# Last group of layer 1: activation left in PSUM, gh by ScalarE, weight patterns one step sooner and their low parts on two engines

## The chip, the cores and the metric

The kernel runs on one core of one Trainium2 chip. The metric is the device time of one execution in microseconds. The engines are named as in the profile: PE is TensorE (matmuls), DVE is VectorE, ACT is ScalarE, POOL is GpSimd, and SP is SyncE, which only issues transfers here.

## The reference

Three stages follow one another. The first is a linear attention with a decaying state over 768 positions, for 4 sequences and 8 heads of 48 channels:

```python
cur = np.einsum('bhd,bhe->bhde', u[None] * kt, vt)
y[:, :, t] = np.einsum('bhd,bhde->bhe', rt, state + cur)
state = w[None, :, :, None] * state + np.einsum('bhd,bhe->bhde', kt, vt)
```

Its result, 3072 tokens by 384 channels, goes through two layers of the same shape (384 to 2048 to 384) with two activations:

```python
h = x @ w_in;  g = h * (1.0 / (1.0 + np.exp(-1.702 * h)));  x = g @ w_out        # layer 1
h = x @ w_in;  sp = np.log1p(np.exp(np.minimum(h, 20.0)));  out = (h * np.tanh(sp)) @ w_out   # layer 2
```

The weights come as 64-bit floats, all the rest as 32-bit floats.

## The kernel before

**Precision.** A 32-bit operand is split in two: a high part, which is a copy rounded to the format of PE's faster 32-bit matmul, and a low part, which is the operand minus the high part. A product is then three matmuls: high by high, low by high, high by low (`PASSES`).

**Weights.** The two matrices of a layer are cut into 16 tiles of 128 partitions by 768 columns. `Layer` brings one tile in five steps. `fetch` loads the raw 64-bit words (SP issues it). `bits` puts together the 32-bit pattern from the two halves of each word, in three DVE instructions: part 0 (L110), part 1 (L116), part 2 (L119). `high` (L142, ACT) copies the pattern into the high part, `low` (L149, POOL) subtracts. A loaded raw tile lies in one of three buffers (two of the tag `raw`, one of `x2_5`), a pattern in one of two of the tag `wv`, and the parts in one of 16 buffers, which the 16 tiles of layer 1 fill: tile m of layer 2 gets its place when tile m of layer 1 was used for the last time.

**Order.** The schedule is manual: each engine runs its instructions in the order of the program, and a wait stands where an instruction needs a result or a buffer of another engine. The tokens are worked through in 6 groups of 512. For a group and a tile m, `product_in` (L544, 9 matmuls) makes h(m) in one of two PSUM buffers, the activation gives g(m), it is split into gh and gl, and `product_out` (L657, 9 matmuls) adds it to three accumulators in PSUM. In groups 0 to 4 of layer 1 the loop also carries the attention of later tokens (units A, kv, y, the masks L385 and the diagonals L358), and in groups 1 to 4 the range check of the weights: each tile of both layers is loaded a second time and read by two ACT instructions, L133 and L135, one in each step, 64 in all.

**The last group of layer 1** (the loop at L751 and after, g = 5) has no attention. In its step m PE runs `product_in` of m and, from m = 1 to 13, `product_out` of m - 1 (`close_tile`); tiles 13 to 15 are closed behind the loop. ACT writes the activation to SBUF (gf, L767), DVE makes gh (a cast, L768) and gl (L769). In the same steps the weights of layer 2 are prepared: `bits` of m - 1, `high` and `low` of m - 2, `fetch` of m + 1. In steps 6, 8 and 10 one third of the first group's input of layer 2 is split (`split_x2`, L581 on DVE and L582 on POOL).

**Layer 2** (`Second`) goes by units u = 16 g + m, in pairs. `inp` makes k(u) into one of the same two PSUM buffers and reads it with ACT (s, L496) and DVE (y, L497); `act` does the rest of the activation for a pair (L506 and L507 on ACT with a change of tables before each, L508 on DVE); `split`, one pair later, gives bh (L520) and bl (L521); `out` (L534) is the second product, four units behind. The tags `s`, `y`, `gh` and `gl` have two buffers each of 128 by 1024. The order at the start is k(0), k(1), `product_out` of tiles 13 to 15, k(2), k(3), and then one k and one out in turn. `late_work` says what else is issued behind which unit: here `bits`, `high` and `low` of the tiles 13 to 15 that are left, and the split of the next group.

Of the kernel before, what the change touches and what calls it, by code (L numbers as in the profile page):

```python
# [17 lines left out]
P = 128  # L18
# [7 lines left out]
NF = 16  # L26
# [9 lines left out]
NB = 2  # L36
# [18 lines left out]
class Layer:  # L55
# [27 lines left out]
    def bits(self, m, part=None):  # L83

        if not 0 <= m < NF:
            return
        if part is None:
            for k in range(3):
                self.bits(m, k)
            return  # L90
        V = self.nc.vector
        raw = self.raw[m]
        if not self.wide:
            self.v[m] = raw
            return
        if part == 0:
            pool, tag, bufs = self.patslot(m)
            self.v[m] = pool.tile([P, 768], I32, tag=tag, name=f"wv{self.tag}_{m}", bufs=bufs)
        v = self.v[m]
        L, H = raw[:, :, 0], raw[:, :, 1]  # L100
        if part == 0:
            if self.general:
                V.tensor_scalar(out=v, in0=H, scalar1=0x7FFFFFFF, scalar2=None, op0=ALU.bitwise_and)
                V.tensor_scalar(out=v.bitcast(F32), in0=v.bitcast(F32), scalar1=F_MIN, scalar2=F_MAX,
                                op0=ALU.max, op1=ALU.min)
                V.tensor_scalar(out=v, in0=v, scalar1=4, scalar2=1, op0=ALU.logical_shift_left,
                                op1=ALU.logical_shift_right)
# [33 lines left out]
        w = self.t[m] = self.wpool.tile([P, 2, 768], F32R, tag="wt", name=f"w{self.tag}_{m}")  # L141
        self.nc.scalar.activation(out=w[:, 0, :], in_=self.v[m].bitcast(F32), func=AF.Copy)  # L142

    def low(self, m, half=None):
        if not 0 <= m < NF:
            return
        sl = slice(0, 768) if half is None else slice(384 * half, 384 * half + 384)
        w = self.t[m]
        self.nc.gpsimd.tensor_tensor(out=w[:, 1, sl], in0=self.v[m][:, sl].bitcast(F32), in1=w[:, 0, sl].bitcast(F32),  # L149
                                     op=ALU.subtract)  # L150

    def win(self, m, part, kt):
        return self.t[m][:, part, 128 * kt:128 * kt + 128]
# [395 lines left out]
def feed_forward(tc, ctx, ins, out, w_sb, chk, consts, general):  # L549
    nc = tc.nc  # L550
    chan, tok, wch, ub, w1, w2, cst = ins
    NG = len(GROUPS)
    starts = [sum(GROUPS[:g]) for g in range(NG)]
    V, A = nc.vector, nc.scalar

    wpool = ctx.enter_context(tc.tile_pool(name="wpool", bufs=NF))
    spool = ctx.enter_context(tc.tile_pool(name="spool", bufs=2))
    xpool = ctx.enter_context(tc.tile_pool(name="xpool", bufs=2))
    x2pool = ctx.enter_context(tc.tile_pool(name="x2pool", bufs=1))
    hpool = ctx.enter_context(tc.tile_pool(name="hpool", bufs=2, space=PSUM))  # L560

    late = {}

    l1 = Layer(nc, w1, wpool, lambda m: (x2pool, "x2_2", 1) if m % 3 == 2 else (spool, "raw", 2),
               lambda m: (x2pool, "x2_1" if m % 2 else "x2_3", 1), "a", chk, spool, general)
    l2 = Layer(nc, w2, wpool, lambda m: (late["x"], "x2_5", 1) if m % 3 == 1 else (spool, "raw", 2),
               lambda m: (late["x"], "wv", 2), "b", chk, spool, general)
    x2, xs, xs2 = {}, {}, {}

    def new_x(g, tag):  # L570
        n = GROUPS[g]
        return (xpool.tile([P, 3, n], F32R, tag="xh", name=f"xh{tag}{g}"),
                xpool.tile([P, 3, n], F32R, tag="xl", name=f"xl{tag}{g}"))

    def split_x2(g, z):
        if g >= NG:
            return
        if z == 0:
            xs2[g] = new_x(g, "b")
        xh, xl = xs2[g]  # L580
        V.tensor_copy(out=xh[:, z, :], in_=x2[g][:, z, :])  # L581
        nc.gpsimd.tensor_tensor(out=xl[:, z, :], in0=x2[g][:, z, :], in1=xh[:, z, :].bitcast(F32), op=ALU.subtract)  # L582


# [66 lines left out]
    def product_out(g, m, gt):  # L651
        n = GROUPS[g]
        if m == 0:
            acc[g] = [psum.tile([P, 512], F32, tag="acc", name=f"acc{g}_{z}", bufs=3) for z in range(3)]
        for ct in range(3):
            for k, (wz, gz) in enumerate(PASSES):
                nc.tensor.matmul(acc[g][ct][:, :n], lhsT=l1.wout(m, wz, ct), rhs=gt[gz],  # L657
                                 start=m == 0 and k == 0, stop=m == NF - 1 and k == 2,
                                 skip_group_check=True)

    def evacuate(g):
        n = GROUPS[g]
        x2[g] = (x2pool if g < NG - 2 else late["x"]).tile([P, 3, n], F32, tag=f"x2_{g}", name=f"x2_{g}")
        for ct in range(3):
            if ct == 0 or g == NG - 1:
                A.activation(out=x2[g][:, ct, :], in_=acc[g][ct][:, :n], func=AF.Copy)
            else:
                V.tensor_copy(out=x2[g][:, ct, :], in_=acc[g][ct][:, :n])

    def range_check(s):  # L670

        n = s // 2
        lay = lambda n: ((l1, l2)[n // NF], n % NF) if n < 2 * NF else (l2, NF)
        if s == 0:
            l1.check(0, 0)
            l1.check(1, 0)
        la, m = lay(n)
        la.check(m, 1 + s % 2)
        if s % 2 == 0 and n > 0:
            la, m = lay(n + 1)  # L680
            la.check(m, 0)

    pend = None
    d = BARE_TILES
    for g in range(NG - 1):
        n = GROUPS[g]
        for m in range(NF):
# [3 lines left out]
            h = product_in(nc, l1, m, xs[g], n, hpool, f"h{g}_{m}")  # L691
# [6 lines left out]
            gh = gpool.tile([P, n], F32R, tag="gh", name=f"gh{g}_{m}")  # L698
            gl = gpool.tile([P, n], F32R, tag="gl", name=f"gl{g}_{m}", bufs=1 if general else 2)
# [13 lines left out]
            if on and q == 2:  # L713
                unit_x(j)
                at.unit_t(j, 1, V)
                at.bonus(j + 1, 2, V)
            if g:
                range_check((g - 1) * NF + m)
            if g == 0:
                l1.bits(d, 2)  # L720
                d += 1
# [21 lines left out]
    g, n = NG - 1, GROUPS[-1]  # L743
# [4 lines left out]
    def close_tile(m):  # L748
        product_out(g, m, gts.pop(m))

    for m in range(NF):  # L751
        h = product_in(nc, l1, m, xs[g], n, hpool, f"h{g}_{m}")
        if m == 0:

            product_out(*pend)
            ax.close()
            late["x"] = ctx.enter_context(tc.tile_pool(name="x2late", bufs=1))
            bpool = ctx.enter_context(tc.tile_pool(name="bpool", bufs=2))
            evacuate(g - 1)
# [194 lines left out]
```

## Time and profile before

| | |
|---|---|
| median of 3 runs | 963.75 us (963.21 to 963.78) |
| the profiled execution | 960.98 us |
| its span | 959.1 us |
| PE busy | 912.9 us, 95% of the span |
| DVE busy | 501.6 us, 52% |
| ACT busy | 557.4 us, 58% |
| POOL busy | 232.8 us, 24% |
| data read, written | 74.37 MB, 4.72 MB |

The profiled execution is one of its own, and its time is larger than its span by what lies before the first and after the last instruction. Times inside the trace count from the start of the span. An engine's busy time is a mean over stages: attention with layer 1 to about 460 us, the last group of layer 1 to about 540, then layer 2.

### The profile page before, as it was taken

How to read it: one execution, taken by the hardware profiler on the slowest of the kernel's cores; microseconds unless marked ns; L12 is line 12 of the kernel's file. 1: busy time of each engine (PE TensorE's matmuls, PEld its weight loads, DVE VectorE, ACT ScalarE, POOL GpSimd, SP SyncE). 2: the span in 40 equal slices, each digit the busy share in tenths (PEclk: the TensorE clock that was granted, in tenths of full speed). 3: DMA queues.
4: the chain of work that ended last, by engine and by line, in shares of the span. 5: the costliest groups of instructions: out<-in, count | busy, mean ns of one | idle time of the engine just before them, and what ended most of it. 6: DMA issues, size and time to landing. Idle time of an engine off the chain costs nothing.

```text
span 959.1 us, 14032 instructions
## 1 busy us (share of the span) xinstructions
PE 912.9 (95%) x5702; PEld 768.1 (80%) x5702; DVE 501.6 (52%) x673; ACT 557.4 (58%) x869; POOL 232.8 (24%) x193
## 2 busy tenths in 40 slices
PE   4679999999999999999988999999999999999997
PEld 3557787887887877887866788999999999999986
DVE  6697842223322222322599867665555555555553
ACT  3445454556554555554322477777777777777773
POOL 5467743231223222221044202101001010010000
PEclk9799999999999999999999899999999999999999
DMA  8746434534334534322243200000000000000001
GB/s 224 220 144 205 141 108 135 140 122 136 112 107 131 153 114 132 115 92 89 109 162 134 98 1 1 1 33 1 1 33 1 33 1 1 33 1 1 33 1 38
DMA packets 30010, 80.09 MB, mean 84 GB/s; under 512 B 3056, under 2 KB 18672, under 8 KB 29936
## 3 DMA queue, kind: packets, MB, share of 16 engines
q1 hardware_dynamic: 29520, 78.66, 26.2%
q8 instruction: 47, 0.77, 0.3%
q10 hardware_dynamic: 416, 0.45, 0.2%
q14 instruction: 27, 0.22, 0.1%
HBM read 74.37 MB, written 4.72 MB: 82 GB/s over the span
## 4 chain that ended last, share of the span: by engine, by line
PE 80%; DVE 9%; issue 4%; POOL 3%; ACT 2%; DMA 2%; SPq 0%; POOLq 0%; DVEq 0%; ACTq 0%
PE bcc L534 20%; PE k L544 20%; PE acc L657 17%; PE h L544 16%; PE y L444 4%; DVE wvb L110 3%; PE A L381 2%; POOL wa L149 2%; DMA tkv<-in_tok_dram 2%; DVE wvb L116 1%; DVE wvb L119 1%; PE kv L418 1%; DVE bl L521 1%; POOL rkbuf L335 1%; DVE wva L119 0%
## 5 line engine op out<-in xcount | busy, mean ns | idle before, releaser
L534 PE MATMUL bcc<-wb,bh 128*128 128x384 f32 x768 | 211.5, 337 | 0.0
L657 PE MATMUL acc<-gh,wa 128*128 128x512 f32 x576 | 187.8, 407 | 3.7 <-DVE gh L768 3.7
L709 DVE TENSOR_TENSOR gl<-h,gh 128x512 fp32r<-128x512 f32 x80 | 55.3, 691 | 254.9 <-ACT gh L708 254.9
L544 PE MATMUL h<-xha,wa 128*128 128x512 f32 x576 | 180.4, 393 | 7.3 <-POOL wa L149 3.5
L544 PE MATMUL k<-xhb,wb 128*128 128x512 f32 x576 | 179.7, 393 | 2.2 <-ACT gf L767 2.2
L534 PEld LDWEIGHTS bcc<-wb,bh 128*128 128x128 f32 x768 | 140.3, 188 | 4.1
L707 ACT ACTIVATE h<-h 128x512 f32<-128x512 f32 x80 | 46.5, 581 | 163.0 <-PE h L544 163.0
L544 PEld LDWEIGHTS h<-xha,wa 128*128 128x128 f32 x576 | 108.5, 189 | 33.9 <-POOL wa L149 4.6
L657 PEld LDWEIGHTS acc<-gh,wa 128*128 128x128 f32 x576 | 106.1, 190 | 34.1 <-DVE gh L768 6.2
L534 PE MATMUL bcc<-wb,bl 128*128 128x384 f32 x384 | 129.2, 337 | 1.9 <-DVE bl L521 1.9
L544 PEld LDWEIGHTS k<-xhb,wb 128*128 128x128 f32 x576 | 106.8, 188 | 20.6 <-ACT gf L767 2.6
L657 PE MATMUL acc<-gl,wa 128*128 128x512 f32 x288 | 115.7, 402 | 4.3 <-DVE gl L769 2.9
L544 PE MATMUL k<-xlb,wb 128*128 128x512 f32 x288 | 114.1, 396 | 0.0
L544 PE MATMUL h<-xla,wa 128*128 128x512 f32 x288 | 112.9, 392 | 0.0
L497 DVE TENSOR_TENSOR y<-k,s 128x512 f32<-128x512 f32 x96 | 66.1, 691 | 86.3 <-ACT s L496 86.2
L508 DVE SCALAR_TENSOR_TENSOR y<-s,y 128x1024 f32<-128x1024 f32 x48 | 59.9, 1248 | 79.5 <-ACT s L507 79.5
L496 ACT ACTIVATE s<-k 128x512 f32<-128x512 f32 x96 | 57.3, 599 | 63.8 <-PE k L544 63.3
L582 POOL TENSOR_TENSOR xlb<-x,xhb 128x512 fp32r<-128x512 f32 x18 | 24.6, 1368 | 258.0 <-DVE xhb L581 258.0
L534 PEld LDWEIGHTS bcc<-wb,bl 128*128 128x128 f32 x384 | 72.1, 188 | 6.9 <-DVE bl L521 3.1
L506 ACT ACTIVATE s<-s,one 128x1024 f32<-128x1024 f32 x48 | 55.4, 1154 | 32.4 <-DVE y L497 32.3
L358 ACT ACTIVATE Am<-ident,a 128x128 f32<-128x128 f32 x192 | 58.5, 389 | 24.9 <-DVE a L348 24.9
L657 PEld LDWEIGHTS acc<-gl,wa 128*128 128x128 f32 x288 | 55.1, 191 | 20.3 <-DVE gl L769 5.6
(99 smaller groups left out, 1253.2 us busy)
## 6 DMA issues: line engine op xcount, KB each, us to landing
rawa<-in_w_dram SPq DMA_DIRECT2D x16, 768.0 KB, 4.5
chka<-in_w_dram SPq DMA_DIRECT2D x16, 768.0 KB, 4.4
chkb<-in_w_dram SPq DMA_DIRECT2D x16, 768.0 KB, 4.2
rawb<-in_w_dram SPq DMA_DIRECT2D x16, 768.0 KB, 4.1
rkbuf<-in_chan_dram SPq DMA_DIRECT2D x48, 192.0 KB, 5.5
tkv<-in_tok_dram SPq DMA_DIRECT2D x24, 384.0 KB, 6.1
tkr<-in_tok_dram SPq DMA_DIRECT2D x24, 192.0 KB, 5.7
out_dram<-o SPq DMA_DIRECT2D x10, 384.0 KB, 3.0
```

Of the source, the lines that this page charges most:

```text
L110: V.tensor_scalar(out=v, in0=H, scalar1=3, scalar2=0x3FFFFFF8, op0=ALU.logical_shift_left, op1=ALU.bitwise_and)
L358: self.nc.scalar.activation(out=am[:, z, p, :], in_=self.ident, func=AF.Copy, scale=self.a[j][:, 2 * p + z:2 * p + z + 1])
L444: self.nc.tensor.matmul(y[32 * s:32 * s + rows, C * x:C * x + C], lhsT=lhsT, rhs=rhs, start=n == 0, stop=n == len(jobs[s]) - 1, skip_group ...
L496: nc.scalar.activation(out=self.s[:, z, :n], in_=h[:, :n], func=AF.Sigmoid)
L497: nc.vector.tensor_tensor(out=self.y[:, z, :n], in0=h[:, :n], in1=self.s[:, z, :n], op=ALU.mult)
L506: nc.scalar.activation(out=s, in_=s, func=AF.Arctan, scale=-1.0, bias=self.one)
L508: nc.vector.scalar_tensor_tensor(out=y, in0=s, scalar=R2, in1=y, op0=ALU.add, op1=ALU.mult)
L534: self.nc.tensor.matmul(self.acc[g][t][:, :DM], lhsT=gt[gz][:, t * P:t * P + P], rhs=self.lay.wout(m, wz), start=m == 0 and k == 0, stop=m ...
L544: nc.tensor.matmul(h[:, :n], lhsT=lay.win(m, wz, kt), rhs=x[xz][:, kt, :], start=k == 0, stop=k == 8)
L657: nc.tensor.matmul(acc[g][ct][:, :n], lhsT=l1.wout(m, wz, ct), rhs=gt[gz], start=m == 0 and k == 0, stop=m == NF - 1 and k == 2, skip_grou ...
L707: A.activation(out=h[:, :n], in_=h[:, :n], func=AF.Gelu_apprx_sigmoid)
L709: V.tensor_tensor(out=gl, in0=h[:, :n], in1=gh.bitcast(F32), op=ALU.subtract)
```

## The change

- In the last group of layer 1 the activation is written back into h's PSUM buffer; ACT makes gh from it by a second instruction, and DVE makes gl from h (PSUM) and gh.
- `split_x2` in steps 6, 8 and 10 makes its high part on ACT.
- `bits` of tile m is done in step m, its parts 0 and 1 ahead of gl and part 2 behind it; all 16 patterns are made in the loop. `fetch` is issued for m + 3. `high` and `low` stay at m - 2 but are issued ahead of the activation; `low` is cut into two halves of 384 columns, the first on POOL, the second on DVE.
- The patterns of layer 2 lie in `wv` for m % 4 = 2, 3, and in the buffers of the tags `s` and `y` of layer 2 for m % 4 = 0, 1.
- In `late_work` the `bits` of tiles 14 and 15 are gone, and `high` and `low` of 14 and 15 come at units 7 and 9 instead of 9 and 11.
- The range checks of groups 1 to 4 go one in each step, but two in the steps 7 and 15 of a group, until the 64 are done.
- The second accumulator of group 4 is copied out by ACT instead of DVE.

```diff
-    def low(self, m, half=None):
+    def low(self, m, half=None, eng=None):
...
+        eng = eng or self.nc.gpsimd
         sl = slice(0, 768) if half is None else slice(384 * half, 384 * half + 384)
         w = self.t[m]
-        self.nc.gpsimd.tensor_tensor(out=w[:, 1, sl], in0=self.v[m][:, sl].bitcast(F32), in1=w[:, 0, sl].bitcast(F32),
-                                     op=ALU.subtract)
+        eng.tensor_tensor(out=w[:, 1, sl], in0=self.v[m][:, sl].bitcast(F32), in1=w[:, 0, sl].bitcast(F32),
+                          op=ALU.subtract)
...
     l2 = Layer(nc, w2, wpool, lambda m: (late["x"], "x2_5", 1) if m % 3 == 1 else (spool, "raw", 2),
-               lambda m: (late["x"], "wv", 2), "b", chk, spool, general)
+               lambda m: (late["x"], "wv", 2, 768) if m % 4 > 1 else (late["b"], "sy"[m % 4], 2, NB * 512), "b", chk, spool, general)
...
-        V.tensor_copy(out=xh[:, z, :], in_=x2[g][:, z, :])
+        if act:
+            A.activation(out=xh[:, z, :], in_=x2[g][:, z, :], func=AF.Copy)
+        else:
+            V.tensor_copy(out=xh[:, z, :], in_=x2[g][:, z, :])
...
-            if ct == 0 or g == NG - 1:
+            if ct == 0 or g == NG - 1 or (ct == 1 and g == NG - 2):
...
-            if g:
-                range_check((g - 1) * NF + m)
+
+            for _ in range(0 if g == 0 else 2 if m % 8 == 7 else 1):
+                range_check(checked)
+                checked += 1
...
         if m == 0:
 
+            A.activation(out=h[:, :n], in_=h[:, :n], func=AF.Gelu_apprx_sigmoid)
             product_out(*pend)
...
-            evacuate(g - 1)
...
-        gf = bpool.tile([P, NB, 512], F32, tag="s", name=f"gf{g}_{m}")[:, 0, :n]
+
+        if m < NF - 1:
+            l2.high(m - 2)
+            l2.low(m - 2, 0)
+            l2.low(m - 2, 1, V)
+        if m:
+            l2.bits(m, 0)
+            l2.bits(m, 1)
...
-        A.activation(out=gf, in_=h[:, :n], func=AF.Gelu_apprx_sigmoid)
-        V.tensor_copy(out=gh, in_=gf)
-        V.tensor_tensor(out=gl, in0=gf, in1=gh.bitcast(F32), op=ALU.subtract)
+        if m:
+            A.activation(out=h[:, :n], in_=h[:, :n], func=AF.Gelu_apprx_sigmoid)
+        A.activation(out=gh, in_=h[:, :n], func=AF.Copy)
+        if m == 0:
+            evacuate(g - 1)
+        V.tensor_tensor(out=gl, in0=h[:, :n], in1=gh.bitcast(F32), op=ALU.subtract)
         gts[m] = (gh, gl)
-        if m < NF - 1:
-            l2.bits(m - 1)
-            l2.high(m - 2)
-            l2.low(m - 2)
-            if m >= 2:
-                l2.fetch(m + 1)
+        if m == 0:
+            l2.bits(0)
+        else:
+            l2.bits(m, 2)
+        if m < NF - 3:
+            l2.fetch(m + 3)
         if 0 < m < NF - 2:
             close_tile(m - 1)
         if m in (6, 8, 10):
-            split_x2(0, m // 2 - 3)
+            split_x2(0, m // 2 - 3, True)
...
-    for u, f, *a in ((5, l2.high, 13), (5, l2.low, 13), (5, l2.bits, 14, 0), (5, l2.bits, 14, 1),
-                     (7, l2.bits, 14, 2), (7, l2.bits, 15, 0),
-                     (9, l2.high, 14), (9, l2.low, 14), (9, l2.bits, 15, 1), (9, l2.bits, 15, 2),
-                     (11, l2.high, 15), (11, l2.low, 15), (11, split_x2, 1, 0),
-                     (13, split_x2, 1, 1), (13, split_x2, 1, 2)):
+    for u, f, *a in ((5, l2.high, 13), (5, l2.low, 13), (7, l2.high, 14), (7, l2.low, 14), (9, l2.high, 15), (9, l2.low, 15),
+                     (11, split_x2, 1, 0), (13, split_x2, 1, 1), (13, split_x2, 1, 2)):
```

## Rows read from the trace of the kernel before

**Rows 1.** Windows: stretch, its length, busy time (count) by engine, PEclk, DMA, GB/s.

```profile
489.60:541.97 52.37, 43.55 (x164) 31.76 (x162) 51.05 (x52) 13.55 (x21) 22.49 (x13) 0.93 0.40 137
541.97:552.12 10.15, 10.12 (x37) 8.17 (x38) 6.36 (x8) 6.46 (x8) 1.44 (x1) 0.83 0.17 68
...
600.00:900.00 300.00, 300.00 (x1506) 271.71 (x1505) 170.07 (x214) 222.34 (x225) 18.15 (x14) 1.00 0.04 14
```

**Rows 2.** Chain of waits, 489 to 496 us: share of the stretch by line.

```profile
by line: DVE wvb L110 32.1%; DVE wvb L119 27.4%; issue 18.1%; DVE wvb L116 13.9%; DVE gh L768 10.0%; DVE gl L769 1.4%; DVEq L769 0.3%
```

**Rows 3.** Timeline of PE: start, length, instruction, count, idle before and its releaser.

```profile
469.20 0.62 PE L657 MATMUL acc<-gh,wa 128*128 128x512 f32 x2
...
485.52 0.62 PE L657 MATMUL acc<-gh,wa 128*128 128x512 f32 x2
...
542.00 0.74 PE L544 MATMUL k<-xhb,wb 128*128 128x512 f32 x2 [2.18 <-ACT gf L767]
...
551.96 0.62 PE L544 MATMUL k<-xhb,wb 128*128 128x512 f32 x2
```

**Rows 4.** Timeline of DVE: its first L110, one step, and a gl.

```profile
471.11 0.55 DVE L110 TENSOR_SCALAR wvb<-rawb 128x768 int32<-128x768 int32 x1
...
490.25 0.69 DVE L769 TENSOR_TENSOR gl<-gf,gh 128x512 fp32r<-128x512 f32 x1
490.86 2.24 DVE L110 TENSOR_SCALAR wvb<-rawb 128x768 int32<-128x768 int32 x1
...
494.13 0.96 DVE L119 SCALAR_TENSOR_TENSOR wvb<-rawb,wvb 128x768 int32<-128x768 int32 x1
495.01 0.42 DVE L768 CAST gh<-gf 128x512 fp32r<-128x512 f32 x1
495.53 0.69 DVE L769 TENSOR_TENSOR gl<-gf,gh 128x512 fp32r<-128x512 f32 x1
...
501.03 1.65 DVE L769 TENSOR_TENSOR gl<-gf,gh 128x512 fp32r<-128x512 f32 x1
```

**Rows 5.** Timeline of POOL in the same steps.

```profile
490.83 1.84 POOL L149 TENSOR_TENSOR wb<-wvb,wb 128x768 fp32r<-128x768 f32 x1 [3.36 <-ACT wb L142]
...
500.74 1.39 POOL L582 TENSOR_TENSOR xlb<-x,xhb 128x512 fp32r<-128x512 f32 x1 [2.82 <-DVE xhb L581]
```

**Rows 6.** Groups by line and shape: busy us and mean ns, idle before.

```profile
L709 DVE TENSOR_TENSOR gl<-h,gh 128x512 fp32r<-128x512 f32 x80 | 55.3, 691 | 254.9 <-ACT gh L708 254.9
...
L454 DVE TENSOR_TENSOR T<-T,wp 112x384 f32<-112x384 f32 x3 | 1.7, 560 | 0.0
...
L149 POOL TENSOR_TENSOR wa<-wva,wa 128x384 fp32r<-128x384 f32 x4 | 4.2, 1079 | 7.9 <-ACT wa L142 7.9
...
L708 ACT ACTIVATE gh<-h 128x512 fp32r<-128x512 f32 x80 | 47.9, 598 | 2.6
...
L142 ACT ACTIVATE wb<-wvb 128x768 fp32r<-128x768 f32 x16 | 13.5, 845 | 44.3 <-DVE wvb L119 44.3
```

**Rows 7.** The page's DMA issues: count, KB each, us to landing.

```profile
chkb<-in_w_dram SPq DMA_DIRECT2D x16, 768.0 KB, 4.2
```

**Rows 8.** Timeline of ACT, DVE and PE around a check, the masks and y.

```profile
441.94 1.00 ACT L135 ACTIVATE chkb<-chkb,one 128x768 f32<-128x768 f32 x1
...
447.11 1.34 DVE L385 COPY_PREDICATED Am<-triNone,A 128x512 f32<-128x512 uint8 x2
...
450.35 0.86 PE L444 MATMUL y<-rkbuf,T 112*32 112x128 f32 x24
```

**Rows 9.** Timeline of POOL, DVE and PE at the start of layer 2.

```profile
564.44 2.32 POOL L149 TENSOR_TENSOR wb<-wvb,wb 128x768 fp32r<-128x768 f32 x1 [21.03 <-ACT wb L142]
...
565.16 2.68 DVE L521 SCALAR_TENSOR_TENSOR bl<-y,bh 128x1024 fp32r<-128x1024 f32 x1
...
567.90 0.44 PE L534 MATMUL bcc<-wb,bl 128*128 128x384 f32 x1 [1.04 <-DVE bl L521]
...
585.34 0.45 PE L534 MATMUL bcc<-wb,bl 128*128 128x384 f32 x1 [0.45 <-DVE bl L521]
```

More of the change, by code (lines that the diff above doesn't have):

```diff
@@ L96, in bits @@
         if part == 0:
-            pool, tag, bufs = self.patslot(m)
-            self.v[m] = pool.tile([P, 768], I32, tag=tag, name=f"wv{self.tag}_{m}", bufs=bufs)
+            pool, tag, bufs, size = self.patslot(m)
+            self.v[m] = pool.tile([P, size], I32, tag=tag, name=f"wv{self.tag}_{m}", bufs=bufs)[:, :768]
         v = self.v[m]
@@ L564, in feed_forward @@
     l1 = Layer(nc, w1, wpool, lambda m: (x2pool, "x2_2", 1) if m % 3 == 2 else (spool, "raw", 2),
-               lambda m: (x2pool, "x2_1" if m % 2 else "x2_3", 1), "a", chk, spool, general)
+               lambda m: (x2pool, "x2_1" if m % 2 else "x2_3", 1, 768), "a", chk, spool, general)
     l2 = Layer(nc, w2, wpool, lambda m: (late["x"], "x2_5", 1) if m % 3 == 1 else (spool, "raw", 2),
-               lambda m: (late["x"], "wv", 2), "b", chk, spool, general)
+               lambda m: (late["x"], "wv", 2, 768) if m % 4 > 1 else (late["b"], "sy"[m % 4], 2, NB * 512), "b", chk, spool, general)
     x2, xs, xs2 = {}, {}, {}
@@ L573, in new_x, with split_x2 @@
                 xpool.tile([P, 3, n], F32R, tag="xl", name=f"xl{tag}{g}"))
-    def split_x2(g, z):
+    def split_x2(g, z, act=False):
         if g >= NG:
@@ L668, in evacuate, with range_check @@
                 V.tensor_copy(out=x2[g][:, ct, :], in_=acc[g][ct][:, :n])
[L670 to L674, printed above, removed]
+    checks = [(lay, m, part) for lay in (l1, l2) for m in range(NF) for part in (1, 2)]
+    def range_check(n):
+        if n >= len(checks):
+            return
+        if n == 0:
             l1.check(0, 0)
             l1.check(1, 0)
[L677 to L681, printed above, removed]
+        lay, m, part = checks[n]
+        lay.check(m, part)
+        if part == 1 and 0 < n < len(checks) - 2:
+            lay, m, part = checks[n + 2]
+            lay.check(m, 0)
     pend = None
     d = BARE_TILES
+    checked = 0
     for g in range(NG - 1):
@@ L757, in feed_forward @@
             late["x"] = ctx.enter_context(tc.tile_pool(name="x2late", bufs=1))
-            bpool = ctx.enter_context(tc.tile_pool(name="bpool", bufs=2))
-            evacuate(g - 1)
+            bpool = late["b"] = ctx.enter_context(tc.tile_pool(name="bpool", bufs=2))
             l2.fetch(1)
             second = Second(nc, l2, bpool, hpool, xpool, xs2, consts)
-        gf = bpool.tile([P, NB, 512], F32, tag="s", name=f"gf{g}_{m}")[:, 0, :n]
+        if m < NF - 1:
[5 more added lines that the diff above has]
+            l2.bits(m, 1)
         if m % NB == 0:
```

## The prediction

> **What bounds the kernel now.** First the page's slices: PE is at 9 tenths nearly everywhere except at the start and in the slices around 490 to 560 us, where DVE rises to 8 and 9. Then the windows [rows 1]: from 600 to 900 us PE is busy 300.00 of 300 us at full clock, so whatever is gained before 600 moves the end by as much. From 489.60 to 541.97 PE is busy 43.55 of 52.37 us at a granted clock of 0.93, and DVE 51.05. So the last group of layer 1 is bound by DVE. The chain of waits says the same: in a step of that group all its pieces but issue are DVE's, first L110 [rows 2].
>
> How long is a step? On PE, out(0) (product_out of tile 0) starts at 469.20 and out(4) at 485.52, without idle [rows 3]: 16.32/4 = 4.08 us, 18 matmuls of 0.227. On DVE, from one L769 to the next, 495.53 - 490.25 = 5.28 [rows 4]: gl 0.61, then L110, L116 and L119 4.15, the cast 0.52. L110 alone takes 0.55 at 471.11, and 2.24 here [rows 4]; POOL's L149 runs from 490.83 to 492.67 [rows 5], and L110 ends at 493.10, 0.43 after it. So 1.7 us of each DVE step is L110 held up by POOL. In the three steps with split_x2 the same happens to gl (L769, 1.65 instead of 0.69 [rows 4] beside L582 [rows 5]), and the step is longer still. PE waits for it; at 542.00 it waits 2.18 for ACT's gf [rows 3], and the stretch after that runs at clock 0.83 [rows 1]. The last product of layer 1 ends, and k(2) starts, at 551.96 [rows 3].
>
> **Part by part, loop.** *DVE's work in a step.* The cast goes to ACT. gl now reads h in PSUM; 80 such instructions (L709) took 0.691 in the mean [rows 6], in a part of the kernel where POOL works a lot. It stays 0.61 start to start. Added is half of low: 384 columns, nearest row L454, 0.560 [rows 6], so 0.48 to the next start. L110 0.58, L116 and L119 0.88 each when the next does not depend on them (494.13 to 495.01 [rows 4]). Sum 0.48 + 0.58 + 0.88 + 0.61 + 0.88 = 3.43.
> *POOL's half of low*: 1.08 (L149 with 384 columns [rows 6]). L110 and L769 (two operands in SBUF) were held up by POOL, L709 (one in PSUM) never: its mean is that of one alone. So I let the half hold up L110, L116, L119 and low, but not gl. Where does it fall? POOL starts when ACT's high(m-2) is done (0.845 [rows 6]); high needs a buffer of the weights, free when out(m-2) ends. Counted from the end of gl(m-2), out(m-2) ends about 1.6 to 2.0 later, high 0.9 after that: 2.5 to 3. At that point DVE is in L116 or at the start of the next gl (0.88 + 0.48 + 0.58 + 0.88 = 2.83). So POOL runs beside gl, which it does not hold up, and the step is 3.43 + 1.08 - 0.61 = 3.90. If the half lay beside nothing: 4.51. I take 3.90, since the phase corrects itself: with DVE late, POOL starts earlier in DVE's step, and the reverse. It is below PE's 4.08, so PE sets the step.
> *ACT*: high 0.85, activation 0.6, gh 0.60, in three steps 0.6 for split_x2: at most 2.65 of 4.08, hidden; cover gone, it costs nothing until 1.4 more is added.
> *split_x2*: L582 (1.39 [rows 5]) stays on POOL. Beside it the step is 1.3 longer, three times, 3.9. Worked through, DVE has a lead of about 0.9 at step 6, loses it there, and PE waits about 0.5 at steps 8 and 10: 1.0 (bounds 0 and 3.9).
> *fetch* two steps sooner: SP waits for the buffer of tile m, then 4.2 us of transfer (by a load of the same size [rows 7]), against three steps, 12 us. Nothing. Tile 1's pattern is now wanted at step 1, at about 471; its load needs only SP, which is free earlier, as the checks end half a group sooner.
> *range_check*, two instead of one in 7 steps of groups 1 to 4: one more is 1.00 on ACT (L135). The masks then end at 448.45 + 1.0 [rows 8]; y starts at 450.35. Nothing.
>
> **The tail of the loop.** Patterns 14 and 15 move in from the second layer. Let out(12) start at S. PE reaches k(0) at S + 3 x 2.04 = 6.1, but its PSUM buffer (two) is now held until gl(14); gl(12) ends at about S - 0.1, two DVE steps later (3.90 and 3.5) is S + 7.4: wait 1.3. k(1) needs gl(15), 0.88 + 0.58 + 0.88 + 0.61 = 2.95 later, S + 10.4; PE is there at 9.5: wait 0.9. I add one clock dip: the window 541.97 to 552.12 lost 0.17 x 10.15 = 1.7 [rows 1].
> So k(2) starts at 469.20 + 12 x 4.08 + 1.0 + (8 x 2.04 = 16.3) + 2.2 + 1.7 = 539.4, against 551.96: 12.6 gained.
>
> **What it gives back.** Patterns 0, 1, 4, 5 ... now lie in buffers of the tags s and y. Pattern 13 takes one of the two y buffers, and its last readers, high(13) and low(13), are issued at u = 5, behind Second.inp(4), which asks for a third y tile. So DVE's y(4) must wait until POOL has read pattern 13; queued behind it on DVE are y(5), split of pair (2,3) and L508, and PE's k(6) waits for y(4) too, since it frees k(4)'s PSUM buffer. Times of before: low(13) starts at 564.44 [rows 9] and takes 1.84 when nothing holds it up (as at 490.83 [rows 5]): 566.3. y(4) ends at 566.9; PE got to k(6) at 567.90 - 1.04 - 2.04 - 0.3 = 564.5 [rows 9], so it waits 2.5. bl then comes at 566.3 + 0.61 + 0.61 + 0.72 + 1.1 = 569.3, k(6) ends at 569.0: 0.4 more. Before, the wait here was 1.04 (L521 2.68 beside POOL [rows 9]): 1.9 worse. The two later waits of 0.45 (the first is at 585.34 [rows 9]), of tiles 14 and 15, stay, perhaps 0.3 longer as they come sooner: 2.2 in all. And 2.5 us without work should bring a dip as at 542, 1.7. Bounds: 0 (no such wait) and 5. I take 3.9.
>
> **Sum**: 12.6 - 3.9 = 8.7. The profiled execution took 960.98 for a span of 959.1; it becomes 952.3. The median of the runs shown, 963.75, lies 2.77 above that execution; the same 8.7 off it gives 955.0, which I forecast. Its own range is 951 to 958 (dips absent, or splits at 3.9).
>
> **Rivals.** *A: the halves do not run together, and POOL's is always on DVE's path.* Then the step is 4.51, 0.43 over PE's in 12 steps, 5.2, and the splits cost 3.9 less the lead 0.9: 8.2 instead of 1.0, so 1.5 gained, 962.2; if half of it lies beside gl, 959. For it: L110 and L769 were each held up to the end of POOL's instruction. Against: where POOL starts. By the Trainium skill (SBUF — State Buffer, section "SBUF: two separate sides") VectorE with two SBUF inputs or in a 2-port mode and GpSimd take an exclusive lock in turn, so that low's halves cannot overlap; the rows on L110 agree, 0.43 after POOL's end; no row of before shows two halves of low at once. By that rule the halves would take 1.56 in turn, which is the 4.51 above.
> *B: y(4) finds another buffer.* Then the 3.9 are not given back: 951.1. For it: I read the wait from the buffers, no trace shows it. Against: of the tag's two buffers one holds the tile of pair (2,3) then, the other pattern 13.
> *C, slower: double checks hold up attention.* Where a second check waits for its transfer, ACT's queue stands: diagonal, the next activation and the masks behind it. The cover is 450.35 - 448.45 = 1.9, of which the check itself takes 1.0. From a wait of 2.15 on, 7 steps lose over 1.25 each, more than 8.7; with 2.5 it is 7 x 1.6 = 11.2, 966.3. Against: the load is issued two checks earlier, over 8 us, and takes 4.2 [rows 7].
>
> **Chances**: forecast 0.68; A 0.14; B 0.13; C 0.03; anything else about as before or slower 0.02. The range 949 to 961 leaves out most of A's upper half, C and little else. A measurement of this kernel tells 0.2% (1.9 us) from no change. Faster: forecast 0.68, B 0.13 and half of A, 0.88; same: the other half of A, 0.07; slower 0.05, C and the rest.
>
> **What would show it.** Right: L110 near 0.55 to 1.0 in the loop, gl at 0.69 beside POOL, PE steps of 4.1 to step 7, k(2) near 539, PE waiting at k(0), k(1) and k(6), y(4) starting as POOL's low(13) ends. Wrong: PE steps of 4.5 with waits for gl (A), no idle PE at k(6) (B), idle PE between 140 and 460 us (C). The forecast fails altogether if DVE's step is over 5 us.

## The result, and the profile after

The changed kernel took 951.32 us in the median of 4 runs (950.81 to 952.32), the kernel before 963.48 (962.29 to 963.78) beside it. The ratio is 0.9877, with an interval of [0.986, 0.9894]: 12.2 us faster, where 8.7 were forecast. The profiled execution took 950.81 us, for a span of 948.8.

To find the place I cut both traces at three points: out(0), k(2) and the end.

| us | before | after | forecast |
|---|---|---|---|
| out(0) to k(2) | 82.76 | 68.13 | 70.2 |
| k(2) to the end of the span | 407.14 | 409.33 | 411.0 |
| sum | 489.90 | 477.46 | 481.2 |

The loop gained 14.6 (12.6 forecast), and layer 2 gave back 2.2 (3.9 forecast). The sum, 12.4, is the whole of what the medians show. It is taken from out(0) on because the start of an execution is not the same twice: out(0) came at 469.20 before [rows 3] and at 471.34 after, and in the eleven experiments anywhere from 469.1 to 474.0. All of that spread lies ahead of group 1, where no edit does anything: ACT's first gh of group 1 comes at 136.82 before and at 138.96 after, and out(0) comes 332.37 to 332.39 later in every kernel of this case.

The loop no longer waits for DVE. Windows of the changed kernel (columns as in [rows 1]):

```profile
489.60:541.97 52.37, 50.40 (x221) 40.76 (x220) 46.49 (x57) 28.97 (x42) 16.79 (x12) 1.00 0.40 135
541.97:552.12 10.15, 9.44 (x46) 8.04 (x45) 2.61 (x3) 8.86 (x10) 0.00 (x0) 1.00 0.01 2
```

Against [rows 1], PE is busy 50.40 instead of 43.55 of the first 52.37 us, and its granted clock is 1.00 in both stretches, where it was 0.93 and 0.83.

PE's timeline in the loop and around the joint of the two layers (start, length, instruction, idle before and its releaser):

```profile
471.34 0.39 PE L661 MATMUL acc<-gh,wa 128*128 128x512 f32 x1
...
487.66 0.61 PE L661 MATMUL acc<-gh,wa 128*128 128x512 f32 x2
...
503.98 0.39 PE L661 MATMUL acc<-gh,wa 128*128 128x512 f32 x1
...
508.43 0.39 PE L661 MATMUL acc<-gh,wa 128*128 128x512 f32 x1
...
520.67 0.62 PE L661 MATMUL acc<-gh,wa 128*128 128x512 f32 x2
...
528.25 0.73 PE L545 MATMUL k<-xhb,wb 128*128 128x512 f32 x2 [1.30 <-DVE gl L788]
...
531.18 0.73 PE L545 MATMUL k<-xhb,wb 128*128 128x512 f32 x2 [0.59 <-DVE gl L788]
...
539.47 0.39 PE L545 MATMUL k<-xhb,wb 128*128 128x512 f32 x1
...
544.42 0.73 PE L545 MATMUL k<-xhb,wb 128*128 128x512 f32 x2 [0.71 <-DVE y L498]
...
555.00 0.73 PE L545 MATMUL k<-xhb,wb 128*128 128x512 f32 x2 [1.93 <-DVE y L498]
...
559.54 0.63 PE L545 MATMUL k<-xhb,wb 128*128 128x512 f32 x2
```

From out(0) to out(4) it is 16.32, and again to out(8) at 503.98: 4.08 a step, PE's own pace, kept up to out(12) at 520.67 but for one step of 4.45 (503.98 to 508.43). Then come the two waits that were forecast, k(0) 1.30 and k(1) 0.59. k(2), the line at 539.47, is where the forecast put it (539.4), but partly by luck, since this execution's out(0) was 2.1 late.

DVE's timeline in two steps of the loop, and its y(4) of layer 2:

```profile
478.39 0.69 DVE L788 TENSOR_TENSOR gl<-h,gh 128x512 fp32r<-128x512 f32 x1
478.99 1.43 DVE L119 SCALAR_TENSOR_TENSOR wvb<-rawb,wvb 128x768 int32<-128x768 int32 x1
...
482.27 0.68 DVE L788 TENSOR_TENSOR gl<-h,gh 128x512 fp32r<-128x512 f32 x1
482.87 1.62 DVE L119 SCALAR_TENSOR_TENSOR wvb<-rawb,wvb 128x768 int32<-128x768 int32 x1
484.42 0.55 DVE L150 TENSOR_TENSOR wb<-wvb,wb 128x384 fp32r<-128x384 f32 x1
484.89 0.55 DVE L110 TENSOR_SCALAR wvb<-rawb 128x768 int32<-128x768 int32 x1
...
486.35 0.68 DVE L788 TENSOR_TENSOR gl<-h,gh 128x512 fp32r<-128x512 f32 x1
...
554.25 1.29 DVE L498 TENSOR_TENSOR y<-k,s 128x512 f32<-128x512 f32 x2 [4.27 <-POOL wb L150]
```

and POOL beside them, with the ACT instruction that it waits for:

```profile
478.59 1.02 POOL L150 TENSOR_TENSOR wb<-wvb,wb 128x384 fp32r<-128x384 f32 x1 [2.86 <-ACT wb L142]
...
481.74 0.85 ACT L142 ACTIVATE wb<-wvb 128x768 fp32r<-128x768 f32 x1 [0.83 <-PE acc L661]
...
482.67 1.01 POOL L150 TENSOR_TENSOR wb<-wvb,wb 128x384 fp32r<-128x384 f32 x1 [3.06 <-ACT wb L142]
...
552.40 1.82 POOL L150 TENSOR_TENSOR wb<-wvb,wb 128x768 fp32r<-128x768 f32 x1 [27.55 <-ACT wb L142]
```

L110, which took 2.24 in [rows 4], takes 0.55. POOL's half begins in the middle of gl (482.67 against 482.27) and gl keeps its 0.68; L119, behind it, is held to 1.62 instead of 0.96. The step is 482.27 - 478.39 = 3.88 once, and 4.08 next, though DVE has no idle time in either. The difference is the hold: POOL's half began 0.20 behind gl in the first and 0.40 behind it in the second, so more of it was left when L119 came, which was held for 0.47 and then for 0.66. POOL waits for ACT's high, and high for PE's product, so POOL keeps PE's pace, and DVE's step grows until it keeps it too. The 3.90 that was worked out is met on the way there; it is not a step that DVE keeps.

Lower down stands the give-back: POOL's low(13) begins at 552.40 and lasts 1.82, DVE, idle for 4.27, begins y(4) at 554.25, 0.03 behind POOL's end, and PE's k(6) has waited 1.93 at 555.00.

The chain of waits from 482 to 487 us in the changed kernel:

```profile
by line: DVE wvb L116 38.3%; DVE wvb L119 30.8%; DVE gl L788 24.1%; DVE wvb L110 9.6%; DVE wb L150 9.4%; issue 0.5%
```

It still names only DVE, since it was followed back from a DVE instruction. That PE does not wait there is seen only in PE's own rows above.

### The profile page after: what moved, and what is told of

Same layout as the page of the kernel before. It is cut to its first block, busy times and chain, and to the rows that moved or that the text cites. A ratio compares the mean times of both kernels' runs of the same rounds, so it can differ in the third digit from the quotient of the medians.

```text
span 948.8 us, 14030 instructions
## 1 busy us (share of the span) xinstructions
PE 911.7 (96%) x5702; PEld 769.9 (81%) x5702; DVE 479.5 (51%) x666; ACT 570.3 (60%) x889; POOL 222.4 (23%) x193
## 3 DMA queue, kind: packets, MB, share of 16 engines
HBM read 74.37 MB, written 4.72 MB: 83 GB/s over the span
## 4 chain that ended last, share of the span: by engine, by line
PE 79%; DVE 9%; issue 5%; POOL 4%; ACT 1%; DMA 1%; POOLq 0%; DVEq 0%; ACTq 0%; SPq 0%
PE bcc L535 20%; PE k L545 20%; PE acc L661 16%; PE h L545 16%; PE y L445 4%; PE A L382 2%; DVE wvb L119 2%; POOL wa L150 2%; DVE wvb L116 2%; PE kv L419 1%; DVE wb L150 1%; DVE wvb L110 1%; DVE gl L788 1%; DVE bl L522 1%; POOL rkbuf L336 1%
## 5 line engine op out<-in xcount | busy, mean ns | idle before, releaser
L545 PE MATMUL h<-xha,wa 128*128 128x512 f32 x576 | 182.4, 397 | 5.7 <-POOL wa L150 3.5
L661 PE MATMUL acc<-gh,wa 128*128 128x512 f32 x576 | 184.3, 401 | 0.0
L661 PE MATMUL acc<-gl,wa 128*128 128x512 f32 x288 | 113.5, 394 | 1.2 <-DVE gl L716 1.1
```

Of the source, the lines that this page charges most:

```text
L545: nc.tensor.matmul(h[:, :n], lhsT=lay.win(m, wz, kt), rhs=x[xz][:, kt, :], start=k == 0, stop=k == 8)
```

## The experiments

The first four start from the changed kernel and take one part of it away; the next three change one later place; two do one part alone in the kernel before; two put together what came out better. The table has the median, the ratio to the kernel before of the same chip (963.72, 963.48 or 963.93 us) with its interval, and the two stretches of the profiled execution.

| kernel | us | ratio | out(0) to k(2) | k(2) to end |
|---|---|---|---|---|
| x_pool | 954.41 | 0.99 [0.9883, 0.9916] | 70.25 | 410.09 |
| x_dve | 951.5 | 0.9872 [0.9856, 0.9889] | 66.46 | 410.11 |
| x_order | 958.91 | 0.9938 [0.9919, 0.9957] | 74.54 | 409.48 |
| x_sbuf | 954.1 | 0.9897 [0.9877, 0.9917] | 70.67 | 409.13 |
| tail | 950.29 | 0.9863 [0.9838, 0.9889] | 65.97 | 409.24 |
| y_free | 950.08 | 0.9859 [0.9833, 0.9886] | 68.16 | 406.81 |
| checks_old | 953.24 | 0.9888 [0.9858, 0.9918] | 68.15 | 410.54 |
| b_psum | 959.87 | 0.9957 [0.9939, 0.9974] | 77.51 | 407.03 |
| b_low | 958.2 | 0.9945 [0.9927, 0.9963] | 75.84 | 408.09 |
| tail_y | 946.2 | 0.9831 [0.9812, 0.985] | 65.97 | 407.22 |
| best | 944.39 | 0.9806 [0.9785, 0.9826] | 65.62 | 405.17 |

Single places are worth 2 us or so, as much as the start varies; for them the stretches decide, and the times only agree.

**x_pool: low whole on POOL again.**

```diff
-            l2.low(m - 2, 0)
-            l2.low(m - 2, 1, V)
+            l2.low(m - 2)
```

> The changed kernel with low whole on POOL (768 columns) instead of half on POOL and half on DVE. Theory: a step of the last group lasts as long as DVE's own instructions plus that part of POOL's low that does not lie beside gl. DVE alone 2.95, POOL 1.84 of which 0.61 beside gl: 4.18, just over PE's 4.08, and the three split steps get no slack: the stretch from out(0) to k(2), 68.13 in the changed kernel, becomes 70 to 73, the time 953 to 956. Rival, DVE's own work alone decides: DVE has 0.48 less to do in a step, so 68 and 951 or less.

Measured: 70.25, 2.1 more than with the halves. POOL and DVE in one step of x_pool:

```profile
488.26 1.84 POOL L150 TENSOR_TENSOR wb<-wvb,wb 128x768 fp32r<-128x768 f32 x1 [2.23 <-ACT wb L142]
```

```profile
488.83 2.08 DVE L119 SCALAR_TENSOR_TENSOR wvb<-rawb,wvb 128x768 int32<-128x768 int32 x1
```

POOL's instruction is 0.8 longer and L119 grows from 0.96 to 2.08, but DVE has 0.48 less work of its own. Outside the three steps with split_x2 its step is 3.96 to 4.07, just below PE's 4.08 and not the 4.18 expected. The 2.1 are lost in those three (4.96 to 5.06 each against 4.71 or 4.72 with the halves, and PE waits 0.48 for gl twice) and at k(0), where PE waits 1.64 instead of 1.30. The new order with gl from PSUM already hides most of a whole low.

**x_dve: low whole on DVE.**

```diff
-            l2.low(m - 2, 0)
-            l2.low(m - 2, 1, V)
+            l2.low(m - 2, None, V)
```

> The changed kernel with low whole on DVE. Theory: DVE 3.43 - 0.48 + 0.88 = 3.83 in a step and nothing of POOL in it but the three splits; below 4.08, so the stretch from out(0) to k(2) stays at 68 to 68.5 and the time at 951. Rival, the sharing between the two engines is what pays: DVE gets 0.4 more per step, falls behind in the split steps, and the stretch becomes 71 or more, 954 or more.

Measured: 66.46, 1.7 less than with the halves, though DVE has more to do. DVE in one step:

```profile
484.96 0.69 DVE L787 TENSOR_TENSOR gl<-h,gh 128x512 fp32r<-128x512 f32 x1
...
486.43 0.95 DVE L150 TENSOR_TENSOR wb<-wvb,wb 128x768 fp32r<-128x768 f32 x1
...
488.76 0.69 DVE L787 TENSOR_TENSOR gl<-h,gh 128x512 fp32r<-128x512 f32 x1
```

The step is 3.80. A whole low costs DVE 0.95, a half 0.55 and then up to 0.8 of being held by the other half. So sharing low between the two engines bought nothing that DVE alone would not have given. PE keeps 4.08 a step up to out(12), with no loss in the split steps, and does not wait at k(0). The median is the same all the same. Layer 2 took 0.8 longer, since PE waited 2.52 at k(6) and its clock dipped behind that (see checks_old); the 0.9 that is left is less than the start varies.

**x_order: the old places of bits, high, low and fetch.**

```diff
-        if m < NF - 1:
-            l2.high(m - 2)
...
+        if m < NF - 1:
+            l2.bits(m - 1)
+            l2.high(m - 2)
+            l2.low(m - 2, 0)
+            l2.low(m - 2, 1, V)
+            if m >= 2:
+                l2.fetch(m + 1)
```

> The changed kernel with bits, high, low and fetch of layer 2 back in the place that they had before (bits of m - 1 behind gl, then high and low of m - 2, patterns 14 and 15 in the second layer), but gh by ACT, gl from PSUM and low shared. Theory: POOL's half now starts while DVE is in L110 or L116, which it holds up, and DVE's half waits for it too: step 3.55 + 1.08 = 4.6, stretch from out(0) to k(2) 75 to 79, time 958 to 962. Rival, only the sum of DVE's work counts and the order does not: 68 to 70, 951 to 953.

Measured: 74.54, 6.4 more, the largest part of all. DVE in one step, then POOL:

```profile
487.46 0.68 DVE L781 TENSOR_TENSOR gl<-h,gh 128x512 fp32r<-128x512 f32 x1
488.06 0.55 DVE L110 TENSOR_SCALAR wvb<-rawb 128x768 int32<-128x768 int32 x1
488.64 1.65 DVE L116 SCALAR_TENSOR_TENSOR wvb<-rawb,wvb 128x768 int32<-128x768 int32 x1
490.33 0.96 DVE L119 SCALAR_TENSOR_TENSOR wvb<-rawb,wvb 128x768 int32<-128x768 int32 x1
...
491.68 0.68 DVE L781 TENSOR_TENSOR gl<-h,gh 128x512 fp32r<-128x512 f32 x1
```

```profile
488.03 1.45 POOL L150 TENSOR_TENSOR wb<-wvb,wb 128x384 fp32r<-128x384 f32 x1 [2.77 <-ACT wb L142]
```

The half now falls behind gl, not beside it, and holds L116 for 1.65 - 0.96 = 0.69. DVE's own work in this order is 3.53, 0.10 more than in the new one, since L119 now comes directly behind L116, whose result it needs. The step is 3.53 + 0.69 = 4.22, not the 4.6 expected, and 0.14 over PE's 4.08. Of the 6.4, 1.9 come up to out(12), with the split steps; 4.5 come behind it, where k(0) waits 1.89 and k(1) 2.03 for gl, and the granted clock is 0.94 and 0.89 in the two ten-microsecond windows from 530 to 550 us against 1.00 in the changed kernel.

**x_sbuf: the activation in SBUF again**, with ACT's gh kept. The patterns that lay in the buffers of `s` move to those of `y`.

```diff
-            A.activation(out=h[:, :n], in_=h[:, :n], func=AF.Gelu_apprx_sigmoid)
-        A.activation(out=gh, in_=h[:, :n], func=AF.Copy)
+        gf = bpool.tile([P, NB, 512], F32, tag="s", name=f"gf{g}_{m}")[:, 0, :n]
+        A.activation(out=gf, in_=h[:, :n], func=AF.Gelu_apprx_sigmoid)
+        A.activation(out=gh, in_=gf, func=AF.Copy)
...
-        V.tensor_tensor(out=gl, in0=h[:, :n], in1=gh.bitcast(F32), op=ALU.subtract)
+        V.tensor_tensor(out=gl, in0=gf, in1=gh.bitcast(F32), op=ALU.subtract)
```

> The changed kernel with the activation written to SBUF as before, gh by ACT from there and gl from two SBUF operands; the patterns that lay in s and y all lie in y, so that s is free for it. Theory: gl is now held up by POOL like the other DVE instructions, POOL's half lies beside nothing: step 3.43 + 1.08 = 4.5, the stretch from out(0) to k(2) 73 to 77, time 956 to 960. Rival, where the activation lies does not matter as long as ACT makes gh: 68, 951.3.

Measured: 70.67, so less than expected. DVE, then POOL:

```profile
484.45 0.68 DVE L787 TENSOR_TENSOR gl<-gf,gh 128x512 fp32r<-128x512 f32 x1
485.05 1.77 DVE L119 SCALAR_TENSOR_TENSOR wvb<-rawb,wvb 128x768 int32<-128x768 int32 x1
...
488.67 1.50 DVE L787 TENSOR_TENSOR gl<-gf,gh 128x512 fp32r<-128x512 f32 x1
```

```profile
484.49 1.52 POOL L150 TENSOR_TENSOR wb<-wvb,wb 128x384 fp32r<-128x384 f32 x1 [2.71 <-ACT wb L142]
488.57 1.05 POOL L150 TENSOR_TENSOR wb<-wvb,wb 128x384 fp32r<-128x384 f32 x1 [2.56 <-ACT wb L142]
```

In these two steps whoever begins first holds the other. At 484.45 gl is 0.04 ahead and POOL's half lasts 1.52; at 488.57 POOL is 0.10 ahead and gl lasts 1.50, that is 0.82 over its 0.68. The step, 488.67 - 484.45, is again 4.22: without a gl that reads PSUM there is nothing for POOL's half to lie beside. So in the new order the PSUM operand is what makes the ordinary step fit into 4.08.

The 70.67 is the sum of a loss and a gain. PE in x_sbuf, whose out(0) is at 472.00:

```profile
526.35 0.61 PE L661 MATMUL acc<-gh,wa 128*128 128x512 f32 x2
...
532.47 0.61 PE L545 MATMUL k<-xhb,wb 128*128 128x512 f32 x2
```

Up to out(12), at 526.35, it takes 54.35, where the changed kernel takes 49.33: 5.0 lost. Behind it k(0) comes 6.12 later, three products at PE's pace. PE, late already, waits neither there nor at k(1): gl(15) ends 8.2 behind out(12), where it is 10.5 in the changed kernel. That gives back 2.5.

**tail: patterns 14 and 15 behind gl(14) and gl(15).** In the last two steps all DVE work on patterns is issued behind gl.

```diff
-        if m:
+        if 0 < m < NF - 2:
             l2.bits(m, 0)
             l2.bits(m, 1)
...
+        elif m == NF - 2:
+            l2.bits(m, 0)
+            l2.bits(m, 1)
+        else:
+            l2.bits(m - 1, 2)
+            l2.bits(m)
```

> The changed kernel with gl of tiles 14 and 15 ahead of the bits of patterns 14 and 15 on DVE (order: gl 14, bits 14 parts 0 and 1, gl 15, bits 14 part 2, bits 15). Theory: PE's waits at k(0) and k(1), 1.30 and 0.59, are for gl held behind these patterns; they go, and the patterns are not missed before unit 7. Stretch from out(0) to k(2) 66.2 instead of 68.13, time 949.4. Rival: y(0) and y(1) come later behind the patterns, PE waits for them at k(2) or k(4) instead, the time stays at 951.

Measured: 65.97; PE's waits at k(0) and k(1) are gone, so they were due to the patterns queued ahead of gl.

**y_free: pattern 13 read before layer 2 asks for its buffer.**

```diff
         close_tile(m)
+    l2.high(13)
+    l2.low(13)
     second.split()
...
-    for u, f, *a in ((5, l2.high, 13), (5, l2.low, 13), (7, l2.high, 14),
+    for u, f, *a in ((7, l2.high, 14),
```

> The changed kernel with high and low of tile 13 issued behind the last product_out of layer 1, ahead of split of pair (0,1), instead of at unit 5. Theory: y(4) no longer waits for POOL's low(13); PE's wait of 1.93 at k(6) goes, k(2) to the end becomes 407.4 instead of 409.3, the time 949.4. Rival: at k(6) ACT (its changes of tables) is as late as y(4) was, or low(13) holds up bl of pair (0,1) instead: 409 and 951.

Measured: k(2) to the end 406.81, as before the change (407.14). PE in y_free has no wait at k(6) left:

```profile
545.01 0.50 PE L545 MATMUL k<-xhb,wb 128*128 128x512 f32 x1 [0.78 <-DVE y L498]
...
564.71 0.44 PE L535 MATMUL bcc<-wb,bl 128*128 128x384 f32 x1 [0.45 <-DVE bl L522]
```

**checks_old: one range check per step of groups 1 to 4.** All checks are still run; they end half a group later.

```diff
-            for _ in range(0 if g == 0 else 2 if m % 8 == 7 else 1):
+            for _ in range(1 if g else 0):
```

> The changed kernel with one range check in each step of groups 1 to 4, as before (the last one at step 15 of group 4). Theory: the checks are beside ACT's path in every step, nothing changes: 951.3 within 1, out(0) within the spread of the other kernels (469 to 473.5). Rival (double checks hold up attention): out(0) 2 to 3 earlier, 948.5. Other rival (the early end of the checks is what lets tile 1 land in time): bits of tile 1 late, 952 or more.

Measured: from ACT's first gh of group 1 to its last of group 4 it is 324.87 us here (141.63 to 466.50), and 324.87 or 324.88 in every other kernel of this case, the kernel before (136.82 to 461.69) among them. The second checks cost nothing. The median is even 1.9 higher, with intervals that overlap. In the profiled execution that comes from elsewhere: it reached out(0) only at 474.01, and the clock fell at k(6). Windows around k(6), first the changed kernel, then checks_old, then x_dve:

```profile
553.00:560.00 7.00, 5.04 (x24) 4.20 (x24) 3.83 (x5) 4.32 (x4) 1.22 (x1) 1.00 0.00 1
```

```profile
555.00:563.00 8.00, 6.07 (x23) 5.18 (x22) 4.15 (x5) 4.64 (x5) 1.82 (x1) 0.79 0.00 1
```

```profile
549.00:556.00 7.00, 4.48 (x14) 3.63 (x14) 3.15 (x5) 3.63 (x4) 1.80 (x1) 0.76 0.00 1
```

PE waited 1.93 there in the changed kernel, 1.94 in checks_old and 2.52 in x_dve. PE's rows at k(6), in the middle of it and at k(7) in checks_old:

```profile
557.68 0.74 PE L545 MATMUL k<-xhb,wb 128*128 128x512 f32 x2 [1.94 <-DVE y L498]
...
559.19 1.05 PE L545 MATMUL k<-xhb,wb 128*128 128x512 f32 x2
...
563.53 0.63 PE L545 MATMUL k<-xhb,wb 128*128 128x512 f32 x2
```

Two matmuls take 1.05 at 559.19 where they take 0.62 at full clock, so part of the window ran at the lower of the two levels of the clock. From k(6) to k(7) it is 4.54 in the changed kernel (555.00 to 559.54), 5.85 in checks_old and 5.82 in x_dve: the dip costs 1.3 in both. x_pool, x_order, x_sbuf and tail wait 1.93 or 1.94 there too and take 4.55 or 4.56, without a dip.

**b_psum: the kernel before with the activation in PSUM and gh by ACT, no more.** The same lines as in x_sbuf, the other way round.

> The kernel before with one part of the change: activation left in PSUM, gh by ACT, gl from PSUM. Theory: the cast's 0.52 leaves DVE's step, 5.28 to 4.76, and gl in the split steps is no longer held up (0.95 each); L110 is still held up by the whole low on POOL. Stretch from out(0) to k(2) 82.76 - 12 x 0.52 - 3 x 0.95, and up to two clock dips fewer: 70.5 to 74, time 952 to 955. Rival, the hold of L110 decides and only its end brings the gain: 80 or more, 961 or more.

Measured: 77.51, 5.3 gained, less than expected. DVE in two steps, with POOL's whole low of the second below:

```profile
486.08 0.68 DVE L768 TENSOR_TENSOR gl<-h,gh 128x512 fp32r<-128x512 f32 x1
...
487.26 2.52 DVE L116 SCALAR_TENSOR_TENSOR wvb<-rawb,wvb 128x768 int32<-128x768 int32 x1
...
490.69 0.68 DVE L768 TENSOR_TENSOR gl<-h,gh 128x512 fp32r<-128x512 f32 x1
```

```profile
487.12 1.84 POOL L149 TENSOR_TENSOR wb<-wvb,wb 128x768 fp32r<-128x768 f32 x1 [2.76 <-ACT wb L142]
```

The cast is gone, but POOL's low still holds up DVE, now at L116, by 2.52 - 0.96 = 1.56: the step is 4.61 and DVE still sets it.

**b_low: the kernel before with low in halves on POOL and DVE**, the same two calls as in the change.

> The kernel before with one part of the change: low in two halves of 384 columns, the first on POOL, the second on DVE, in the old place. Theory: POOL's half holds DVE for 0.79 instead of 1.7, and DVE gets 0.47 more: step 5.28 - 0.9 + 0.47 = 4.85. PE is late from step 5 on, so some 9 steps gain 0.4 and the stretch from out(0) to k(2) is 78 to 80 instead of 82.76, time 959 to 961. Rival, the half on DVE waits for POOL's half and nothing is gained: 82 or more, 963.

Measured: 75.84, 6.9 gained, better than expected. DVE, then POOL:

```profile
492.52 1.38 DVE L110 TENSOR_SCALAR wvb<-rawb 128x768 int32<-128x768 int32 x1
```

```profile
492.04 1.45 POOL L150 TENSOR_TENSOR wb<-wvb,wb 128x384 fp32r<-128x384 f32 x1 [3.37 <-ACT wb L142]
```

A half holds L110 up by 0.83 (1.38 - 0.55) where the whole held it up by 1.69 [rows 4], so a step is 4.81. Each of the two parts alone leaves DVE's step above 4.08, and so do both in the old order (x_order, 4.22). In the new order with gl from PSUM it is below, whether low is in halves or whole (x_pool).

**tail_y and best.** The first joins tail and y_free, the second also puts low whole on DVE everywhere:

```diff
+    l2.low(13, None, V)
...
-            l2.low(m - 2, 0)
-            l2.low(m - 2, 1, V)
+            l2.low(m - 2, None, V)
...
+    for u, f, *a in ((7, l2.high, 14), (7, l2.low, 14, None, V), (9, l2.high, 15), (9, l2.low, 15, None, V),
```

> The changed kernel with both edits of the last two tries: gl of tiles 14 and 15 ahead of the patterns, and high and low of tile 13 ahead of the first split. Theory: they are independent, 1.9 and 2.5 less: out(0) to k(2) 66.0, k(2) to the end 406.8, time 946.8. Rival: with PE earlier at k(2), s(2) and y(2) become later for PE, the wait of 0.7 at k(4) grows by what was gained, and the time is 948.5 or more.

> As tail_y, and low of every tile of layer 2 whole on DVE (POOL keeps only the splits of the inputs). Theory: out(0) to k(2) 65.9, and the two waits of 0.45 for bl, which L149 on POOL holds up, go: k(2) to the end 405.9, time 945.8. Rival: DVE's longer queue (low waits for high on ACT) makes bl as late as POOL did: 406.8 or more, 946.8.

Measured: 946.2 us and 944.39 us (943.58 to 947.29). The intervals of best [0.9785, 0.9826] and of the change [0.986, 0.9894] lie apart, so best beats both kernels. Of PE's waits over 0.3 us between 500 and 600 us one is left in best:

```profile
544.12 0.50 PE L545 MATMUL k<-xhb,wb 128*128 128x512 f32 x1 [0.44 <-DVE y L498]
```

tail_y takes the same 65.97 in the loop as tail and 407.22 in layer 2, where its wait at k(4) grew from 0.71 to 1.07. best is 2.05 shorter than tail_y in layer 2. By PE's starts, 1.4 of it are the two waits of 0.45 for bl, which POOL's lows of tiles 14 and 15 held up. The other 0.6 is the wait at k(4): in tail_y POOL's low(13) held up DVE's bh, which took 2.15 instead of 0.68, and y(2) stood behind it.

```profile
536.25 2.15 DVE L521 TENSOR_SCALAR bh<-y 128x1024 fp32r<-128x1024 f32 x1
```

## Why the prediction was right, and where it was not

**Right in mechanism.** DVE's step was the bound, 1.7 us of it was L110 held up by POOL, and PE's 4.08 took over: PE's rows show it up to out(12). x_order and x_sbuf show that both the place of POOL's half and the PSUM operand are needed for it. That the phase corrects itself is seen in the steps of 3.88 and 4.08, but DVE's step then ends at PE's pace, not at 3.90. The two waits at k(0) and k(1) come from the patterns queued ahead of gl (tail), and the give-back comes from pattern 13's buffer (y_free), as the prediction read them from the code.

**The size, 3.7 too small** (12.4 against 8.7), came from the clock, 3.4, and the split steps, 0.6, less 0.3 that k(0) and k(1) cost more. The ends of matmuls are modelled in the trace, so what a wait costs is taken here from the starts of the products, and it is more than the idle time that the row gives.

- *The granted clock: 3.4 added, 0 came.* Two dips of 1.7 were put in, one at the joint and one at k(6). The changed kernel shows 1.00 in all three windows there. The rows at 0.93 and 0.83 belong to a stretch in which PE was busy only 43.55 of 52.37 us, and to what follows it [rows 1]; the prediction carried their price over to a stretch with single waits. At k(6) the dip came in x_dve, whose wait of 2.52 is the forecast's 2.5, and in one of the six kernels with a wait of 1.93 or 1.94; it cost 1.3, not 1.7. That the changed kernel had none is thus in part chance.
- *split_x2: 1.0 put in, 0.37 measured*, one step of 4.45 instead of 4.08.
- *k(0) and k(1): 1.3 and 0.9 put in.* k(0) came 1.46 late (idle 1.30), k(1) 0.89 late (idle 0.59), and the product behind it 0.13. With 12 x 4.08 + 16.32 + 0.37 that is the whole of the 68.13.
- *Layer 2 without the clock: 2.2 put in, 2.2 measured, but in part by luck.* k(6) and the product behind it lost 2.5 where 2.9 was put in, with 0.4 for bl. The wait for bl before the change (idle 1.04) cost 1.3, which is saved. The two later waits for bl (idle 0.45 each) are as before, where 0.3 more was put in. k(4) and the product behind it lost 0.95, which the prediction had not: DVE was idle for 1.77 there until ACT's s(2) came for y(2).

**The hold by POOL was less than its row.** The prediction charged DVE with the whole row of POOL's half, 1.08. What the rows show is that a DVE instruction is longer by what is left of POOL's row when it begins, less 0.12 to 0.15:

| kernel | held | POOL's row left | longer by |
|---|---|---|---|
| before [rows 4, 5] | L110 | 1.81 | 1.69 |
| b_psum | L116 | 1.70 | 1.56 |
| x_pool | L119 | 1.27 | 1.12 |
| b_low | L110 | 0.97 | 0.83 |
| x_sbuf | gl | 0.95 | 0.82 |
| x_order | L116 | 0.84 | 0.69 |
| the changed kernel | L119 | 0.81 | 0.66 |

The forecast's step did not hang on it, as PE sets that. But rival A did. x_sbuf is its case: POOL's half always on DVE's path makes a step of 4.22, not 4.51. Up to out(12) x_sbuf lost 5.4 against 12 x 4.08, 1.6 in ordinary steps and 3.8 in the split steps, where A had 5.2 and 3.0. A was too dear in the ordinary steps, and the upper end of the range with it.

The held instructions are not only those with two operands in SBUF, as the prediction says of L110: L110 and bh read a single one, and both were held [rows 4, and bh in tail_y].

The Trainium skill says (SBUF — State Buffer, section "SBUF: two separate sides") that VectorE with two SBUF inputs and GpSimd take their shared ports as an exclusive lock, and that whoever starts first keeps it for the whole instruction. The rows of x_sbuf agree on who waits for whom and on the PSUM operand as the way out. They differ in size: the half's row lasts 1.05 there, and gl, begun 0.10 behind it, is longer by 0.82, not by 0.95. Starts 0.03 apart do not tell who is held: in x_order POOL's half at 488.03 is ahead of L110 at 488.06 and is the one held, 1.45 against 0.55 for L110, while in the kernel before L110, also 0.03 behind, was held [rows 4, 5].

**B and C.** The time alone would have spoken for B (no wait for the buffer): 951.32 was measured, and B's price was 951.1, the forecast 955.0. It is refuted by the row of y(4), which begins as POOL's low(13) ends, and by y_free, in which the wait is gone. C (the checks) is refuted by the 324.87 or 324.88 us that groups 1 to 4 take in all kernels.

**Left open:** why the same wait of 1.9 us at k(6) is followed by a lower clock in one execution and not in five others, what of POOL's row is not held against DVE, and what ahead of group 1 makes an execution vary by up to 4.9 us (469.1 to 474.0 for out(0)). None of it was tried.

## What to carry to other kernels

Find the instruction on the bounding engine whose row is longer than the same row elsewhere (L110: 2.24 against 0.55), and ask which other engine's row begins just before it; the remedy may be to move that work, to let it lie beside an instruction with a PSUM operand, or simply to do it on the bounding engine itself, which here gave the shorter loop (x_dve, 66.46 against 68.13). When weight patterns borrow another stage's buffers, look up who reads them last and what is queued behind the first that wants the buffer back. Gains below the spread of an execution's start are read from a stretch between two marks of the trace, not from the total.

## What the hardware showed that was not expected

- POOL's subtract lengthens a DVE instruction that it holds by what is left of POOL's row, less 0.12 to 0.15 us, in seven kernels, with 384 columns and with 768. The hold goes both ways: POOL's half took 1.52 behind a gl with two SBUF operands, and 1.01 or 1.02 beside one that reads PSUM.
- A wait of PE of 1.93 to 1.94 us went with no dip of the granted clock in five executions, and with one (0.79 over 8 us) in a sixth; the dip cost 1.3 us.
